# Turning the attention probabilities of twelve tiles on VectorE and through DRAM, in GpSimd's queue, in place of TensorE transposes

## The chip, the core and the metric

The kernel runs on one core of a Trainium2 chip. The metric is the device time of one execution in microseconds. Before the change the median of three timed runs is 555.21 us (554.4 to 555.64). TensorE (PE in the profile) does the products and the transposes into PSUM, VectorE (DVE) and ScalarE (ACT) empty PSUM and do the arithmetic, GpSimd (POOL) does a few copies and issues some DMAs, SyncE's queue (SP) issues nearly all the others.

## What is computed

Three stages follow each other on 2304 tokens of width 512:

```python
# 1. causal attention in a window of 64, 4 x 8 heads of 64, 576 positions
scores = (q @ k.T) / 8, masked to 0 <= i - j < 64
attn = exp(scores - max); attn /= attn.sum() + 1e-9
x = (attn @ v), heads side by side            # 2304 x 512
# 2. gated product
x = ((x @ w_a) * (x @ w_b)) @ w_out           # inner width 1536
# 3. soft mixture: 32 slots = 8 experts x 4
logits = x @ phi
d = softmax(logits, over tokens); c = softmax(logits, over slots)
slot_out[e] = relu((d.T @ x)[e] @ w1[e]) @ w2[e]
out = c @ slot_out
```

All inputs are float32 in the kernel; `w_a` and `w_b` come as 64-bit floats and are decoded on the chip.

## The kernel before

**Tiles and slots.** The tokens are 18 tiles of 128 (`NTILE`). The gated product of a tile is three units of 512 inner columns (`fg` 0, 1, 2); each unit is two slots, one for `w_a` and one for `w_b`, of 12 (or 24 half as wide) matmuls in `glu` (line 424). ScalarE copies the `a` bank out of PSUM (line 430), VectorE multiplies the `b` bank by it into `g` (line 434). There are 114 slots in all. Slots 0 to 23 are part of a start-up order that is written out as a string; from slot 24 on `run_slot` issues, slot by slot, first the events put at that slot and then the slot's `glu`. TensorE keeps exactly this order (`MANUAL`); the order on the other engines is set by the planner of the tile framework, which goes by program order and by when it reckons an instruction ready.

**Attention of tile t** is put at slots counted from `sA[t]`: queries turned and copied at s-2 and keys at s-1 (`att_q`, `att_k`), scores at s (`att_s`: 32 matmuls of line 259, then eight row minima on VectorE of line 272 and eight exponentials on ScalarE of line 279), division by the row sums at s+1 (`att_n`, line 297), the transposes of the two halves of the heads at s+2 and s+3 (`att_pt`: four TensorE transposes each, line 139 by way of the helper, and one copy out of PSUM, line 307 on ScalarE or line 309 on VectorE), and the product with the values at s+4 (`att_pv`, line 320), whose result is cast by ScalarE (line 325) and split by VectorE (line 327) into the two parts of `x` that `glu` reads. Keys of the half tile before are handed on by a GpSimd copy (line 233). The first slot of tile t's products, `first[t]`, is 6t for tiles 4 to 14, then 90, 92 and 94; `sA[t]` is the smaller of `first[t] - 6` and three slots ahead of the next tile. So tiles 5 to 14 start at 6t - 6 and tiles 15, 16, 17 at 82, 85 and 88, and the values product of each tile stands two slots ahead of the tile's first `glu` at the latest.

**Logits of tile t** are put at slots counted from `R[t]` (24 + 4t for tiles 0 to 7, 57 for tile 8, then 6 more for each tile up to 93 for tile 14). For tiles 2 to 14 `r_b` turns `g` in 32 x 32 squares on VectorE (line 452), writes it to DRAM by four SyncE DMAs (line 458) and reads it back turned by a fifth (line 463); the three parts are put at R-6, R-4 and R-3. `r_l` at R multiplies by `phi` (line 477). `r_k` at R+1 makes both forms of the logits in PSUM (`lt`, lines 497 and 499); VectorE takes their maxima (lines 501, 508 and 532) and ScalarE their exponentials `e`, `co` and `ce` (lines 511, 517 and 535). `r_d` at R+2 transposes `e` on TensorE into `dps`. `lt` and `dps` are tiles of the same single PSUM buffer (`ps_m`, tag "m"), so `dps` waits until every reader of `lt` is done, `ce` being the last. `r_u` at R+3 adds the tile to the slot inputs (line 553).

**Shared buffers.** `ps_t` tag "t" has two PSUM buffers that all transposes use. `ex1` tag "e" has three buffers of 4 KB a partition, used for staging weights at first and then by `r_b`. The project of `w_out` on `phi` in the start-up writes decoded weights to DRAM by twelve DMAs of GpSimd's queue (line 573); all of these are issued before 140 us.

Of the kernel before, what the change touches and what calls it, by code (L numbers as in the profile page):

```python
# [11 lines left out]
F32 = mybir.dt.float32  # L12
# [8 lines left out]
P = 128  # L21
# [46 lines left out]
def swa_glu_softmoe_kernel(  # L68
# [13 lines left out]
    nc = tc.nc  # L82
# [5 lines left out]
    W = 64  # L88
    NTILE = NT // P
# [7 lines left out]
    EPS = 1.0e-9  # L97
    NFIRST = 4
    NLAST = 3
    N_EX1 = 3  # L100
    N_EX2 = 7
    EARLY = 6
# [3 lines left out]
    dram = ctx.enter_context(tc.tile_pool(name="dram", bufs=1, space=bass.MemoryType.DRAM))  # L106
# [5 lines left out]
    small = ctx.enter_context(tc.tile_pool(name="small", bufs=3))  # L112
    ex1 = ctx.enter_context(tc.tile_pool(name="ex1", bufs=N_EX1))

# [23 lines left out]
    def transpose(o, i):  # L138
        nc.tensor.transpose(o, i, ident)  # L139
# [41 lines left out]
    att = att_stack.enter_context(tc.tile_pool(name="att", bufs=2))  # L181
# [116 lines left out]

    def att_pt(t, hh):
        st = sts[t]  # L300
        tp = ps_t.tile([P, 4, P], F32, tag="t", name="tp")
        for u in range(4):
            transpose(tp[:, u], st["pr"][hh][:, u])
        yield
        pT = att.tile([P, 4, P], F32, tag="pT", name="pT", bufs=3)
        if hh == 0 or t <= NFIRST:
            nc.scalar.copy(out=pT, in_=tp)  # L307
        else:
            nc.vector.tensor_copy(pT, tp)  # L309
        st["pT", hh] = pT  # L310

    def att_pv(t):
        st = sts[t]
        xps = ps_t.tile([P, 4, P], F32, tag="x", name="xps", bufs=1)
        for b in range(2):
            vt = loaded[t]["b" if b else "a"]
            c = slice(W * b, W * b + W)
            for u in range(4):
                for h in range(2):
                    nc.tensor.matmul(  # L320
                        xps[W * h:W * h + W, u, c], lhsT=vt[:, 2 * u + h, :], rhs=st["pT", h][:, u, c],
                    )
        yield
        x = xp.tile([P, 2, 4, P], F32R, tag="x", name="x")
        nc.scalar.copy(out=x[:, 0], in_=xps)  # L325
        yield
        nc.vector.tensor_tensor(out=x[:, 1], in0=xps, in1=x[:, 0].bitcast(F32), op=ALU.subtract)
        xts[t] = (x[:, 0], x[:, 1])
        del sts[t], loaded[t]


    whi, wlo = {}, {}
    wbufs = {"w0": 8, "w1": 8, "w2": 4, "w3": 4, "e": N_EX1}
    wo_dram = dram.tile([DFF, DM], F32, name="wo_dram")
# [131 lines left out]
    def bank(t, shape, nm):  # L466

        if t < NTILE - 2:
            return ps_m.tile(shape, F32, tag="m", name=nm)
        return ps_s.tile(shape, F32, tag=f"s{t % 2}", name=nm)  # L470
# [19 lines left out]
    def r_k(t):  # L490

        l4 = rst[t, "l4"]
        late = t >= NTILE - NLAST
        lt = bank(t, [P, P + NS], "lt")
# [103 lines left out]
    def both(t0, tag):  # L598

        n = min(4, NTILE - NLAST - t0) if t0 < NTILE - NLAST else NLAST  # L600
        c = p2.tile([P, 4, 4, NS], F32R, tag=tag, name="c4")
# [57 lines left out]
    def fetch(n=0):  # L659

        while nxt[0] < len(order):
            i = nxt[1] % len(slots)
            if nxt[1] >= len(slots) and slots[i][1] in ("as1", "gT1"):
                nxt[1] += 1
                continue
            if nxt[1] < len(slots):
                if n == 0:
                    return
                n -= 1
            elif not all(k in used for k in held[i]):  # L670
                return
            nxt[1] += 1
            pool, tag = slots[i]
            bufs = pool_bufs.get(tag)
            nh = slot_halves.get(tag, 2)
            x = pool.tile([P, 512 * nh], F32, tag=tag, name="xw", bufs=bufs)
            held[i] = []
            h = 0
            while h < nh and nxt[0] < len(order):
                key = order[nxt[0]]  # L680
                src, (r0, nr), (c0, ncol), pair = source(key)
                two = pair and h + 1 < nh
                if key[0] == "1":
                    ncol *= 1 + two
                else:
                    nr *= 1 + two
                nh2 = 1 + two
                nc.sync.dma_start(
                    out=x[:, 512 * h:512 * (h + nh2)].rearrange("p (c d) -> p c d", d=ncol),
                    in_=src[r0:r0 + nr, c0:c0 + ncol].rearrange("(c p) d -> p c d", p=P),  # L690
                )
                for j in range(nh2):
                    key = order[nxt[0]]
                    exw[key] = x[:, 512 * (h + j):512 * (h + j + 1)]
                    held[i].append(key)
                    nxt[0] += 1
                h += nh2

    def use(key):
        used.add(key)  # L700
        return exw[key]


    units = [(0, 0), (1, 0), (0, 1), (1, 1), (2, 0), (2, 1), (3, 0), (3, 1)] + [(t, 2) for t in range(NFIRST)]
    for t in range(NFIRST, NTILE - NLAST):
        units += [(t, fg) for fg in range(NFG)]
    LAST = range(NTILE - NLAST, NTILE)
    units += [(t, fg) for fg in range(NFG - 1) for t in LAST]
    units += [(t, NFG - 1, (h,)) for h in range(2) for t in LAST]
    NSLOT = 2 * len(units)  # L710
    events = {n: [] for n in range(NSLOT + 40)}

    def at(n, f, *a):
        events[n].append((f, a))

    first = {}
# [3 lines left out]
        done[t, fg] = 2 * i + 1  # L720
    sA = {}
    for t in range(NTILE - 1, NFIRST - 1, -1):
        sA[t] = min(first[t] - 6, sA.get(t + 1, NSLOT) - 3)
    lastA = sA[NTILE - 1] + 5
    by_squares = [t for t in range(2, NTILE - NLAST) if done[t, NFG - 1] + 2 < lastA]
    R = {}
    for t in range(NTILE - NLAST):
        R[t] = max(done[t, NFG - 1] + (4 if t in by_squares else 3), R[t - 1] + 4 if t else 24)
    for t in range(NFIRST, NTILE):
        s = sA[t]  # L730
        at(s, att_s, t)
        at(s + 1, att_n, t, 0)
        at(s + 1, att_n, t, 1)
        at(s + 2, att_pt, t, 0)
        at(s + 3, att_pt, t, 1)
        at(s + 4, att_pv, t)
        at(s - 2, att_q, t)
        at(s - 1, att_k, t)
        if t + 1 < NTILE:
            at(s, load, t + 1, "qk")  # L740
            at(s + 5, load, t + 1, "ab")
    for t in range(NTILE):
        if t < NTILE - NLAST:
            r = R[t]
# [15 lines left out]
    a, b, c = LAST  # L760
# [11 lines left out]
    def open_ex():  # L772
# [3 lines left out]
        slots.extend([(p2, "as1")] * 2 + [(p2, "gT1")] * 2)  # L776
        slots.extend([(ex1, "e")] * N_EX1 + [(exs["ex2"], "y")] * N_EX2 + [(exs["ex3"], "z")] * N_EX3 + [(gp, "g"), (xp, "x")])
        slots.extend([(wp, "w0")] * 8 + [(wp, "w1")] * 8 + [(wp, "w2")] * 4 + [(xp, "x")] + [(wp, "w3")] * 4)
        slots.extend([(xp, "x")] * 2 + [(gp, "g")] * 3)
        fetch(4 + N_EX1 + N_EX2 + N_EX3)  # L780
        for t in turns.values():
# [17 lines left out]
    def run_slot(n):  # L799
# [9 lines left out]
        "Ph": lambda _: run(nc.sync.dma_start, phi, moe2_phi.rearrange("(k p) s -> p k s", p=P)), "Ri": lambda _: build_ri(),  # L809
        "Tq": lambda t: load(t, "qk"), "Tv": lambda t: load(t, "ab"), "Aq": att_q, "Ak": att_k, "As": att_s, "An": att_n,  # L810
        "Ap": att_pt, "Av": att_pv, "Sa": partial(stage_w, "a"), "Sb": partial(stage_w, "b"),
        "Da": partial(split_w, "a"), "Db": partial(split_w, "b"), "Ga": lambda t, fg: glu(t, fg, "a"),
        "Gb": lambda t, fg: glu(t, fg, "b"), "Rt": r_t, "Po": project_phi,
# [23 lines left out]
    xps = ps_m.tile([P, DM], F32, tag="m", name="xs")  # L837
    x4 = p2.tile([P, DM], F32, tag="as0", name="x4")
    sps = ps_t.tile([P, KD, NS], F32, tag="x", name="sps", bufs=1)
    with tc.manual_schedule(engines=MANUAL):  # L840
# [16 lines left out]
        for h in range(2):  # L857
            c = slice(DM // 2 * h, DM // 2 * (h + 1))
# [14 lines left out]
    for u in range(2):  # L873
        hps = [ps_ab.tile([P, 512], F32, tag="ab"[n], name=f"h{n}") for n in range(2)]
        for kk in range(KD):
            for n in range(2):
                for e in range(4):
                    nc.tensor.matmul(
                        hps[n][32 * e:32 * e + 32], lhsT=sinT[:, kk],
                        rhs=use(("1", u, kk, e, n)),  # L880
# [129 lines left out]
```

## Time and profile before

| | |
|---|---|
| median of the timed runs | 555.21 us (554.4 to 555.64) |
| the profiled execution | 554.43 us |
| its span, first to last instruction | 552.7 us |
| TensorE busy, mean granted clock | 509.6 us (92%), 0.983 |
| VectorE, ScalarE, GpSimd busy | 310.6, 207.5, 75.5 us |
| DMA moved, mean rate | 103.48 MB, 187 GB/s |
| TensorE transposes of the probabilities, all tiles | 144, 22.7 us busy |

The profile is of one execution. Busy times of matmuls overlap each other, so the time that a group of matmuls takes of TensorE is read from the starts of the instructions around it. In the rows below a line of a timeline has the start in us, the length in us, the engine, the line of the kernel, the operation with its output and inputs, and in brackets how long the engine was idle before it and what ended that.

### The profile page before, as it was taken

To read this page: it belongs to the slowest core of one execution; us is meant where nothing else is said; L and a number is where in the kernel's file an instruction comes from. 1 tells how busy PE (TensorE), PEld (TensorE's weight loads), DVE (VectorE), ACT (ScalarE), POOL (GpSimd) and SP (SyncE) were. 2 spreads that over 40 slices of the span, in tenths; PEclk is the share of its full clock that TensorE was granted. 3 is DMA by queue.
4 is the path that set the end of the run, shared out by engine and by line. 5 is a ranking of instruction groups with operands and counts; after the bars stand their busy time and mean duration, and the time that the engine had idled before them with its cause. 6 is when DMAs were issued, how large, how long until landed. Compare 5 with 4: busy or idle time off the path is not lost.

```text
span 552.7 us, 11931 instructions
## 1 busy us (share of the span) xinstructions
PE 509.6 (92%) x4567; PEld 399.1 (72%) x4567; DVE 310.6 (56%) x888; ACT 207.5 (38%) x636; POOL 75.5 (14%) x110
## 2 busy tenths in 40 slices
PE   4588798989999999999999999999999999989993
PEld 3366576779878888787888878888787778944442
DVE  3999999996556463655646454465554311143123
ACT  5667675455534242324424232342433211132013
POOL 3555556451000000000000000000000000020000
PEclk9789899999999999999999999999999999999997
DMA  9986269565337445453525535255436899799997
GB/s 271 255 242 213 81 219 261 172 187 154 99 92 176 125 126 121 126 117 96 135 81 130 120 92 134 77 135 144 106 84 183 282 365 391 261 329 348 348 357 254
DMA packets 138904, 103.48 MB, mean 187 GB/s; under 512 B 80736, under 2 KB 121696, under 8 KB 138848
## 3 DMA queue, kind: packets, MB, share of 16 engines
q1 hardware_dynamic: 137888, 99.58, 62.1%
q0 software_dynamic: 960, 3.15, 1.5%
q8 instruction: 36, 0.59, 0.4%
q14 instruction: 20, 0.16, 0.1%
HBM read 84.61 MB, written 18.09 MB: 186 GB/s over the span
## 4 chain that ended last, share of the span: by engine, by line
PE 66%; DVE 16%; DMA 10%; issue 3%; ACT 2%; SPq 1%; ACTq 0%; DVEq 0%
PE psb L424 25%; PE psa L424 22%; DMA xw<-in_moe_w_dram 7%; PE lps L477 3%; DVE w L349 3%; PE xps L320 3%; PE ups L553 2%; DVE w L353 2%; PE s L259 2%; PE tp L139 2%; DVE w L343 2%; DVE pr L272 2%; PE tg L139 1%; DVE w L345 1%; DVE rs L291 1%
## 5 line engine op out<-in xcount | busy, mean ns | idle before, releaser
L424 PE MATMUL psb<-whb,x 128*128 128x512 f32 (+1 forms) x576 | 161.5, 349 | 1.8 <-DVE g L434 1.7
L424 PE MATMUL psa<-wha,x 128*128 128x512 f32 (+1 forms) x576 | 160.5, 347 | 2.6 <-ACT wha L397 1.6
L424 PEld LDWEIGHTS psa<-wha,x 128*128 128x128 f32 x576 | 101.5, 190 | 21.5 <-issue 5.7
L424 PEld LDWEIGHTS psb<-whb,x 128*128 128x128 f32 x576 | 101.2, 189 | 21.3 <-issue 6.9
L424 PE MATMUL psa<-wla,x 128*128 128x512 f32 (+1 forms) x288 | 97.2, 338 | 1.2 <-POOL wla L399 1.0
L424 PE MATMUL psb<-wlb,x 128*128 128x512 f32 (+1 forms) x288 | 96.8, 336 | 0.0
L434 DVE TENSOR_TENSOR g<-psb,asb 128x512 f32<-128x512 f32 (+1 forms) x57 | 37.7, 661 | 89.8 <-PE psb L424 76.8
L279 ACT ACTIVATE pr<-pr,nmx 128x128 f32<-128x128 f32 x144 | 55.8, 390 | 47.0 <-DVE nmx L272 47.0
L430 ACT COPY asb<-psa 128x512 f32<-128x512 f32 (+1 forms) x57 | 31.9, 559 | 90.7 <-PE psa L424 90.6
L424 PEld LDWEIGHTS psa<-wla,x 128*128 128x128 f32 x288 | 54.7, 190 | 6.6 <-POOL wla L399 1.7
L424 PEld LDWEIGHTS psb<-wlb,x 128*128 128x128 f32 x288 | 54.7, 190 | 4.4
L233 POOL COPY kTs<-kTs 128x256 f32<-128x256 f32 x17 | 8.2, 482 | 257.3 <-DVE kTs L244 252.7
L325 ACT CAST x<-xps 128x512 fp32r<-128x512 f32 x18 | 10.5, 583 | 50.8 <-PE xps L320 50.8
L259 PE MATMUL s<-kTs,qTs 64*64 64x128 f32 x576 | 23.7, 301 | 5.6 <-DVE nmx L272 3.1
L452 DVE STREAM_TRANSPOSE gq<-g 128x512 f32<-128x512 f32 x39 | 27.6, 708 | 1.0
L279 ACT ACTIVATION_READ_ACCUMULATOR pr<-pr,nmx 128x1 f32 x144 | 27.0, 187 | 0.0
L309 DVE COPY pT<-tp 128x512 f32<-128x512 f32 x13 | 9.0, 690 | 29.5 <-PE tp L139 29.5
L259 PEld LDWEIGHTS s<-kTs,qTs 64*64 64x64 f32 x576 | 18.2, 147 | 9.4 <-issue 4.3
L272 DVE CUSTOM_DVE_ANT_0 pr<-s,masks 128x128 f32<-128x128 f32 x112 | 24.6, 282 | 0.3 <-PE s L259 0.3
L307 ACT COPY pT<-tp 128x512 f32<-128x512 f32 x23 | 13.4, 581 | 27.7 <-PE tp L139 27.7
L139 PE MATMUL tp<-ident,pr 128*128 128x128 f32 x144 | 22.7, 281 | 0.6 <-POOL pr L297 0.6
L139 PEld LDWEIGHTS tp<-ident,pr 128*128 128x128 f32 x144 | 18.1, 144 | 5.5 <-POOL pr L297 1.7
(135 smaller groups left out, 714.0 us busy)
## 6 DMA issues: line engine op xcount, KB each, us to landing
xw<-in_moe_w_dram SPq DMA_DIRECT2D x39, 512.0 KB, 7.3
xw<-in_moe_w_dram SPq DMA_DIRECT2D x50, 256.0 KB, 6.1
gd<-gq SPq DMA_DIRECT2D x156, 64.0 KB, 2.1
gT<-gd SPq DMA_DIRECT2D x39, 256.0 KB, 2.9
st<-in_moe_w_b_dram SPq DMA_DIRECT2D x12, 512.0 KB, 5.6
st<-in_moe_w_a_dram SPq DMA_DIRECT2D x12, 512.0 KB, 5.6
st<-in_moe_w_out_dram SPq DMA_DIRECT2D x12, 512.0 KB, 5.1
out_dram<-ob SPq DMA_DIRECT2D x18, 256.0 KB, 3.2
```

Source lines behind the costliest of these rows:

```text
L139: nc.tensor.transpose(o, i, ident)
L259: nc.tensor.matmul(sps[h][c, u], lhsT=qT[r, u, c], rhs=kTs[r, t % 2, u, W * b:W * b + P],)
L272: nc.vector.tensor_tensor_reduce(out=pr[:, u].rearrange("p (a k) -> p a k", a=2), in0=sps[h][:, u].rearrange("p (a k) -> p a k", a=2), in1 ...
L279: nc.scalar.activation(out=pr[:, u], in_=pr[:, u], func=ACTF.Exp, scale=-1.0, bias=nmx[:, i:i + 1], accum_out=sm[:, i:i + 1],)
L307: nc.scalar.copy(out=pT, in_=tp)
L320: nc.tensor.matmul(xps[W * h:W * h + W, u, c], lhsT=vt[:, 2 * u + h, :], rhs=st["pT", h][:, u, c],)
L349: nc.vector.scalar_tensor_tensor(out=i, in0=hi, scalar=-(1 << 30), in1=i, op0=ALU.bitwise_and, op1=ALU.bitwise_or)
L424: nc.tensor.matmul(ps[:, cols], lhsT=l[:, kk], rhs=r, start=(n == 0), stop=(n == 3 * KD - 1))
L430: nc.scalar.copy(out=asb[:, cols], in_=ps[:, cols])
L434: nc.vector.tensor_tensor(out=gts[t][:, gcols], in0=ps[:, cols], in1=pas.pop((t, fg))[:, cols], op=ALU.mult)
L452: nc.vector.transpose(out=gq.rearrange("p (j c t) -> p c j t", j=4, c=4), in_=gts[t][:, 512 * fg:512 * fg + 512].rearrange("p (c j f) -> p ...
L477: nc.tensor.matmul(lps[32 * i:32 * i + 32].rearrange("p (i t) -> p i t", t=32) if t in by_squares else lps[32 * i:32 * i + 32], lhsT=wphi[ ...
```

## The change

A constant `NPLAIN = 6` divides the tiles. Tiles 0 to 5 keep their transposes on TensorE. For tiles 6 to 17 `att_pt` turns each half of the heads in 32 x 32 squares by one VectorE instruction into one half of a buffer `pq` (from `ex1` tag "e"). When both halves are there, four DMAs of GpSimd's queue write the buffer to a DRAM tile `pd` (32 partitions each, runs of 1 KB), and two more DMAs of the same queue, one for each half of the heads, read it back turned into `pT` (128 partitions, four runs of 512 bytes each). The values product reads `pT` with two runs of 32 columns in place of one of 64. For these tiles `sA` is two slots earlier against `first`, both calls of `att_pt` are put at s+2, the values product at s+6 in place of s+4 and the loads of the next values at s+7 in place of s+5; the end of attention, `lastA`, and the values products stay at the slots where they were.

```diff
--- before.py
+++ after.py
@@ -97,6 +97,7 @@
     EPS = 1.0e-9
     NFIRST = 4
     NLAST = 3
+    NPLAIN = NFIRST + 2
     N_EX1 = 3
     N_EX2 = 7
     EARLY = 6
@@ -298,6 +299,27 @@
 
     def att_pt(t, hh):
         st = sts[t]
+        if t >= NPLAIN:
+
+            if hh == 0:
+                st["pq"] = ex1.tile([P, 4, 2, 4, 32], F32, tag="e", name="pq")
+            pq = st["pq"]
+            nc.vector.transpose(
+                out=pq[:, :, hh].rearrange("p j u q -> p u j q"), in_=st["pr"][hh].rearrange("p u (j k) -> p u j k", j=4)
+            )
+            if hh == 0:
+                return
+            pd = dram.tile([4, 32, 4, 2 * P], F32, tag="pd", name="pd", bufs=2)
+            for i in range(4):
+                nc.gpsimd.dma_start(
+                    out=pd[:, :, i].rearrange("j k e -> k j e"),
+                    in_=pq[32 * i:32 * i + 32].rearrange("p j h u q -> p j (h u q)"),
+                )
+            for h in range(2):
+                pT = att.tile([P, 4, P], F32, tag="pT", name="pT", bufs=3)
+                nc.gpsimd.dma_start(out=pT, in_=pd[:, :, :, P * h:P * h + P].rearrange("j k i e -> (j k) i e"))
+                st["pT", h] = pT.rearrange("p i (u q) -> p u i q", u=4)
+            return
         tp = ps_t.tile([P, 4, P], F32, tag="t", name="tp")
         for u in range(4):
             transpose(tp[:, u], st["pr"][hh][:, u])
@@ -317,9 +339,13 @@
             c = slice(W * b, W * b + W)
             for u in range(4):
                 for h in range(2):
-                    nc.tensor.matmul(
-                        xps[W * h:W * h + W, u, c], lhsT=vt[:, 2 * u + h, :], rhs=st["pT", h][:, u, c],
-                    )
+                    o = xps[W * h:W * h + W, u, c]
+                    if t >= NPLAIN:
+                        o = o.rearrange("p (i q) -> p i q", i=2)
+                        r = st["pT", h][:, u, 2 * b:2 * b + 2]
+                    else:
+                        r = st["pT", h][:, u, c]
+                    nc.tensor.matmul(o, lhsT=vt[:, 2 * u + h, :], rhs=r)
         yield
         x = xp.tile([P, 2, 4, P], F32R, tag="x", name="x")
         nc.scalar.copy(out=x[:, 0], in_=xps)
@@ -720,8 +746,8 @@
         done[t, fg] = 2 * i + 1
     sA = {}
     for t in range(NTILE - 1, NFIRST - 1, -1):
-        sA[t] = min(first[t] - 6, sA.get(t + 1, NSLOT) - 3)
-    lastA = sA[NTILE - 1] + 5
+        sA[t] = min(first[t] - (8 if t >= NPLAIN else 6), sA.get(t + 1, NSLOT) - 3)
+    lastA = sA[NTILE - 1] + 7
     by_squares = [t for t in range(2, NTILE - NLAST) if done[t, NFG - 1] + 2 < lastA]
     R = {}
     for t in range(NTILE - NLAST):
@@ -732,13 +758,14 @@
         at(s + 1, att_n, t, 0)
         at(s + 1, att_n, t, 1)
         at(s + 2, att_pt, t, 0)
-        at(s + 3, att_pt, t, 1)
-        at(s + 4, att_pv, t)
+        late = 2 if t >= NPLAIN else 0
+        at(s + 2 if late else s + 3, att_pt, t, 1)
+        at(s + 4 + late, att_pv, t)
         at(s - 2, att_q, t)
         at(s - 1, att_k, t)
         if t + 1 < NTILE:
             at(s, load, t + 1, "qk")
-            at(s + 5, load, t + 1, "ab")
+            at(s + 5 + late, load, t + 1, "ab")
     for t in range(NTILE):
         if t < NTILE - NLAST:
             r = R[t]
```

## Rows read from the trace of the kernel before

**Rows 1.** Busy time of each engine by stretch (window, length, engines, clock, DMA share, GB/s).

```profile
145.00:430.00 285.00, 281.07 (x2661) 232.36 (x2661) 154.42 (x534) 97.97 (x355) 4.41 (x11) 1.00 0.47 119
```

**Rows 2.** What TensorE waited for in 150:430 (us in total, times, longest).

```profile
PE dps L139 <- ACT ce L535: 1.9, 2, 1.1
PE lps L477 <- DMA gT<-gd: 1.2, 1, 1.2
```

**Rows 3.** Instructions on the tile pr in 170:430 (ns min/median/max, first and last start).

```profile
L139 PE MATMUL tp<-ident,pr x96: 270/272/273, 180.9 to 425.4; 128*128 128x128 f32 x96
```

**Rows 4.** TensorE's timeline around the transposes of tile 10.

```profile
279.48 0.60 PE L139 MATMUL tp<-ident,pr 128*128 128x128 f32 x4
279.83 0.47 PE L424 MATMUL psa<-wha,x 128*128 128x512 f32 x1
...
282.67 0.60 PE L139 MATMUL tp<-ident,pr 128*128 128x128 f32 x4
283.19 0.86 PE L477 MATMUL lps<-gT,wphi 128*32 128x128 f32 x24
...
286.40 0.39 PE L424 MATMUL psb<-wlb,x 128*128 128x512 f32 x1
286.63 0.39 PE L424 MATMUL psb<-whb,x 128*128 128x512 f32 x1
286.95 0.69 PE L320 MATMUL xps<-pT,lda 128*64 128x64 f32 x16
```

**Rows 5.** Costliest groups of the page (busy us, mean ns | idle before).

```profile
L452 DVE STREAM_TRANSPOSE gq<-g 128x512 f32<-128x512 f32 x39 | 27.6, 708 | 1.0
L309 DVE COPY pT<-tp 128x512 f32<-128x512 f32 x13 | 9.0, 690 | 29.5 <-PE tp L139 29.5
```

**Rows 6.** DMAs through DRAM: GpSimd's (issue ns, us to landing), SyncE's (KB, us to landing).

```profile
L573 POOL DMA_DIRECT2D wo_dram<-wo x12: 539/568/1770, 62.9 to 139.7; - x12
DMA to landing us min/median/max: 2.4/4.1/8.5
...
gd<-gq SPq DMA_DIRECT2D x156, 64.0 KB, 2.1
gT<-gd SPq DMA_DIRECT2D x39, 256.0 KB, 2.9
```

**Rows 7.** Slots 52 and 54 on TensorE; the end of tile 10's division on VectorE.

```profile
264.96 0.39 PE L424 MATMUL psa<-wha,x 128*128 128x256 f32 x1
...
272.91 0.48 PE L424 MATMUL psa<-wha,x 128*128 128x512 f32 x1
...
277.59 0.68 DVE L297 TENSOR_TENSOR pr<-pr,rs 128x512 f32<-128x512 f32 x1
```

**Rows 8.** Timeline of slots 82 and 83: scores, `lt`, exponentials, `dps`.

```profile
383.48 1.10 PE L259 MATMUL s<-kTs,qTs 64*64 64x128 f32 x32
384.51 0.49 PE L497 MATMUL lt<-l,ri 128*128 128x128 f32 x2
...
387.94 0.60 PE L139 MATMUL tq<-ident,ldq 128*128 128x128 f32 x4
...
389.23 0.28 ACT L535 ACTIVATE ce<-lt,rm 128x32 f32<-128x32 f32 x1
...
389.66 0.33 PE L139 MATMUL dps<-ident,e 128*128 128x128 f32 x1 [1.13 <-ACT ce L535]
```

**Rows 9.** TensorE's timeline at slot 89.

```profile
417.80 0.33 PE L139 MATMUL dps<-ident,e 128*128 128x128 f32 x1 [0.77 <-ACT ce L535]
```

**Rows 10.** Timeline at slots 37 and 38: `ce` and the transposes ahead of `dps`.

```profile
205.12 0.29 ACT L535 ACTIVATE ce<-lt,rm 128x32 f32<-128x32 f32 x1
...
205.64 0.60 PE L139 MATMUL tp<-ident,pr 128*128 128x128 f32 x4
```

**Rows 11.** One issue of GpSimd's queue in the start-up, and VectorE beside it.

```profile
95.86 1.77 POOL L573 DMA_DIRECT2D wo_dram<-wo  x1 [3.12 <-DVE wo L353]
...
96.08 0.41 DVE L343 TENSOR_SCALAR w<-w 128x512 f32<-128x512 f32 x1
```

## The prediction

> **What bounds the kernel now.** I read the table by stretch first. From 145 to 430 us, which holds all the attention that the change touches, TensorE is busy 281.07 of 285.00 us at a granted clock of 1.00; VectorE is busy 154, ScalarE 98, GpSimd 4, the DMA engines 0.47 [rows 1]. The reader is to see that one engine has no gaps and the others have many. Then I read what TensorE waited for there: the two largest entries are 1.9 us on `dps` and 1.2 us on `lps` [rows 2]. So in this stretch a microsecond taken out of TensorE's order is a microsecond of the span, and one more wait is one lost. What follows 430 us starts from slot 93, where attention ends in both kernels; it moves with it. All sums are made against the profiled execution, 554.43 us, of which the span is 552.7; the median of the runs is 0.78 above it, and I add that at the end.
>
> **Removed: transposes on TensorE.** For tiles 6 to 17, 96 matmuls on `pr` go, in 24 groups of four [rows 3]. A group's busy time overlaps, so I take starts. The group at 279.48 is followed by the next product at 279.83: 0.35 us. The one at 282.67 is followed by `lps` at 283.19: 0.52, but a change from the product to such an f32 group costs 0.09 anyway (the step from 286.63 to 286.95 is 0.32, the ordinary step from 286.40 is 0.23), so 0.43 is saved [rows 4]. Five of the 24 groups are followed directly by a product, the others by another f32 group: 5 x 0.35 + 19 x 0.43 = 9.9 us. TensorE has no gap that could swallow this: **-9.9**.
>
> **Copies and squares.** 24 copies out of PSUM go, half on ScalarE, half on VectorE at 690 ns; 24 turns on VectorE come, bounded by the same shape's 708 ns [rows 5]: net 12 x (2 x 0.71 - 0.69) = 8.8 us more on VectorE, in a stretch where it idles 130 us [rows 1]. At nothing for the sum; it is VectorE's order that can cost, below. The values product reads runs of 32 columns; the `lps` group reads `gT` in the same manner and 24 of its matmuls take 0.8 us [rows 4], so nothing.
>
> **Added: the way through DRAM.** The trace has GpSimd issues of 128 runs only: 0.54 us each at the quickest, landing 2.4 to 8.5 us after, median 4.1 in the busy start-up. SyncE's nearest transfers land in 2.1 (writes of 64 KB from 32 partitions) and 2.9 us (the turned read of 256 KB) [rows 6]. The chain from the end of the division: two turns 1.42; four writes issued 0.54 apart, the last landed 2.4 to 4.1 after its issue, 4.0 to 5.7; two reads, each issue between 0.54 and four times that for its 512 runs (2.16), the last landing 2.9 to 4.1 after its own: 3.4 to 6.3. Together **8.9 to 13.4 us**, nearest to the lower end, since the DMA share is 0.47. If the planner puts a `g` product and a `gq` turn first (0.69 + 0.71), 1.4 more. The cover: tile 10's division ends at 278.27 [rows 7], its values product starts at 286.95 [rows 4], 8.7 us; two slots more (264.96 to 272.91, 7.95) [rows 7], less the 0.8 of removed transposes: **15.8 us**. Tiles 15 to 17 stand only three slots apart, some 12 us, but from the first write's issue to the last read's GpSimd needs at most 5.7 + 2 x 2.16 = 10 of them. So the reads are hidden by the products of four slots, 1 us to spare in the worst sum. Behind the waiting GpSimd issues stands only the copy of the next keys (line 233), which is ready before them. The buffers "e" are asked for four times in six slots and held 4 to 8 us each: three suffice.
>
> **Moved: scores two slots earlier.** This is where I expect loss. New starts are 6t - 8 = 28 to 76 for tiles 6 to 14, then 80, 83, 86. `r_k` of tile t' stands at R+1 = 6t' + 10 from tile 8 on. These meet at slots 58, 64, 70 and 76: scores and logits in one slot. Before, that happens at 82 and 88. What it costs is seen at 82: scores at 383.48, `lt` behind them; VectorE does eight minima before the maxima of `lt`, ScalarE eight exponentials before `e` and the copy of the `a` bank before `ce` (389.23), and only then can `dps` use the buffer: it starts at 389.66, 1.13 us idle behind four query transposes that began at 387.94 [rows 8]. In the new places nothing stands between the product and `dps` (queries are then at s-2, two slots after), so the loss is the whole 389.66 - 387.94 = 1.72. The rest of the slot is alike (the values product stands at 82 too). **+4 x 1.72 = +6.9**; bounds 0.77, the smaller wait, at slot 89 [rows 9], and 2.3 with the key copy or a turn before it. The two old waits, 1.13 and 0.77 [rows 8, 9], go, as no tile now starts at 82 or 88: **-1.9**.
>
> Three more places (slots 28, 40, 52) have the logits one slot after the scores, as slot 37 has now. There `ce` ends at 205.41 and `dps` would be due, without the transposes ahead of it, at 205.64 [rows 10]: 0.2 us to spare. The values product's split (0.69) now comes before the minima at all three, and a turn of `pq` (0.71) fits in front of the last maximum. Bounds 0 and 1.3 each; I take the middle, as either alone exceeds the margin: **+3 x 0.7 = +2.1**.
>
> **Sum:** 554.43 - 9.9 + 6.9 - 1.9 + 2.1 = 551.6; with 0.78 for the median, **552.4 us**. With the bounds (4 x 0.77 to 4 x 2.3; 0 to 3.9) the same case runs from 546.5 to 556.5.
>
> **Rival 1, the new waits do not form.** ScalarE's order is the planner's; if it puts `ce` ahead, or the maxima ahead of the minima, only the removals stay: 554.43 - 9.9 - 1.9 + 0.78 = 543.4. For it: at slot 38 before, the same chain just fits. Against it: at 82 and 88 the same planner made exactly this wait. Chance 0.16.
>
> **Rival 2, the reads come late and the kernel is slower.** Mechanism: the values product (line 320) waits for `pT`, with all TensorE behind it. It decides from a chain of 15.8 us; the forecast's gain of 2.8 over nine tiles (6 to 14) is gone 0.3 us later. Price: one issue in the start-up took 1.77 us [rows 11] where the others take 0.54; at 1.77 for all six and landings of 4.1 the chain is 1.4 + 3 x 1.77 + 4.1 + 1.77 + 1.77 + 4.1 = 18.5, so 2.7 us late in each of nine tiles: 552.4 + 24 = 576. At one such issue and the rest as in the upper sum nothing is late. For it: no run of 512 pieces is in the trace. Against it: that issue ran beside a row of 0.41-us TENSOR_SCALARs on VectorE (the first of them at 96.08) [rows 11], which the stretch from 145 on does not have; and the cover is near twice the lower sum. Chance 0.14.
>
> The Trainium skill ("SBUF — State Buffer", Who interferes with whom) speaks against putting these DMAs on GpSimd: a VectorE copy or TENSOR_SCALAR in its two-port mode shuts GpSimd out for the whole instruction, descriptor writing included, and it advises another queue. By that rule the 1.77 us is explained, and the trace agrees; on VectorE the stretch from 145 us on has such instructions between SBUF tiles on at most 32 columns, so by the rule the issues stay near 0.54 and the sum does not move.
>
> **Rival 3, `lps` waits for its own way through DRAM.** For tiles 8 to 12 `r_b` of the last part stands at R-3 = 54 to 78, the very slots of the new `att_pt`. Two turns (1.42) ahead of `gq`, and 512 KB written and 512 KB read beside `gd` and `gT`, use up a margin of some 3 us. The one such wait in the trace is 1.2 us [rows 2]; five of them give 552.4 + 6 = 558.4, one or two leave it near 555. Chance 0.17.
>
> **How the numbers follow.** Forecast 0.53, rivals 0.16, 0.14, 0.17. A measurement of this kernel can tell about 0.2%, so below 554.1 is faster and above 556.3 slower. Faster: 0.41 of the forecast's 0.53 (554.1 lies some three quarters up its range), rival 1's 0.16, 0.04 of rival 3: 0.61. Same: 0.09 of the forecast, 0.05 of rival 3, 0.01 of rival 2: 0.15. Slower: 0.03, 0.08 and 0.13 of the same three: 0.24. The range: the forecast's bounds with rival 3's full price above, and below down to rival 1 with two of four waits left (545): **545 to 560**. Left out are the rest of rival 1 and nearly all of rival 2, 0.2.
>
> **What would show it.** Right: 48 matmuls on `pr` in place of 144; TensorE's waits led by `dps <- ACT ce`, at four places around 290 to 370 us, 1 to 2 us each; GpSimd's last read landed 2 us or more ahead of line 320, which waits for nothing; six GpSimd issues a tile, the writes near 0.5 us. Wrong: `xps <- DMA pT` among TensorE's waits (rival 2), `lps <- DMA gT` several times (rival 3), no `dps` wait at all (rival 1), or VectorE's turns so late that a `b` bank is not emptied and `psb` waits for line 434.

## The result, and the profile after

The changed kernel takes 549.15 us (547.72 to 549.72) where the kernel before, beside it, takes 554.81 (552.97 to 555.64): a ratio of 0.991, interval 0.989 to 0.993. Measured a second time it was 0.9925, 0.990 to 0.995. The kernel is faster by 4 to 6 us; the forecast was 2.8, with the range 545 to 560.

The profiled execution took 547.72 us, its span is 545.9. Its line numbers are higher than before's: the values product is line 348 (320 before), the logits' product on `gT` 503 (477), `ce` 561 (535); the transpose into `dps` is called in line 569 and recorded at line 140.

The stretch of [rows 1], 5 us shorter, in the table by stretch of the kernel after (window, length, PE, PEld, DVE, ACT and POOL busy with counts, granted clock, DMA share, GB/s):

```profile
145.00:425.00 280.00, 270.98 (x2556) 221.88 (x2555) 159.19 (x547) 90.46 (x341) 48.80 (x83) 1.00 0.64 167
```

GpSimd went from 4 to 49 us and the DMA share from 0.47 to 0.64, the granted clock stayed 1.00. TensorE, which idled 4 us of 285, now idles 9 of 280. What it waited for there, against [rows 2]:

```profile
PE dps L140 <- ACT ce L561: 6.4, 4, 1.6
PE lps L503 <- DMA gT<-gd: 1.6, 2, 1.3
PE psb L450 <- DVE g L460: 0.8, 1, 0.8
```

The four long waits of the forecast are there, and nothing waits for `pT`. The transposes left on `pr` in this stretch, against the 96 of [rows 3] (ns min/median/max, first and last start):

```profile
L140 PE MATMUL tp<-ident,pr x8: 270/272/273, 153.6 to 158.5; 128*128 128x128 f32 x8
```

The costliest groups of the kernel after (busy us, mean ns | idle before), where [rows 6] had only issues of 128 runs, and the landing of its transfers (KB, median us):

```profile
L314 POOL DMA_DIRECT2D pd<-pq x48 | 26.4, 558 | 120.4 <-DVE cst L565 48.0
L320 POOL DMA_DIRECT2D pT<-pd x24 | 18.0, 756 | 40.0 <-DMA pd<-pq 32.0
...
gT<-gd SPq DMA_DIRECT2D x39, 256.0 KB, 3.3
gd<-gq SPq DMA_DIRECT2D x148, 64.0 KB, 2.7
pd<-pq POOLq DMA_DIRECT2D x48, 128.0 KB, 3.2
pT<-pd POOLq DMA_DIRECT2D x24, 256.0 KB, 3.9
```

The `cst` that is named before the writes ends 0.13 us after the turn that they read; the issue follows 0.3 us behind that turn. A read's issue of 512 runs takes 0.76 us, near the lower bound (0.54 to 2.16). Its landing (3.9) is in the forecast's 2.9 to 4.1, the writes' (3.2) in 2.4 to 4.1. The older transfers, [rows 6] 2.1 and 2.9 us, now take 2.7 and 3.3.

The chain of tile 10, from timelines of the kernel after (start, length):

```profile
264.89 0.68 DVE L298 TENSOR_TENSOR pr<-pr,rs 128x512 f32<-128x512 f32 x1
265.61 0.71 DVE L307 STREAM_TRANSPOSE pq<-pr 128x512 f32<-128x512 f32 x1
266.62 2.20 POOL L314 DMA_DIRECT2D pd<-pq  x4 [10.79 <-DVE rm L558]
271.79 1.50 POOL L320 DMA_DIRECT2D pT<-pd  x2 [2.98 <-DMA pd<-pq]
281.51 0.69 PE L348 MATMUL xps<-pT,lda 128*64 128x64 f32 x16
```

The division ends at 265.57, the last packet of the second read lands at 276.38: 10.8 us, and 5.1 more until the product asks. Over the twelve tiles the chain takes 10.1 us (tile 13) to 14.7 (tile 14), and 2.1 us (tile 17) to 7.8 (tile 12) are left over. The semaphore that tells of the landing follows 0.5 to 0.7 us behind the last packet, so by it 1.6 to 7.2 us are left.

**Where the time is.** The first product of slot n is a mark that all these kernels have. Its start, in us from the start of the span, from the timelines of TensorE:

| kernel | slot 24 | 30 | 54 | 78 | 93 | 113 | 24 to 113 |
|---|---|---|---|---|---|---|---|
| before | 148.53 | 174.30 | 272.91 | 368.44 | 433.54 | 483.05 | 334.52 |
| after | 147.16 | 172.96 | 267.46 | 368.20 | 427.34 | 476.85 | 329.69 |
| c_after | 147.39 | 173.18 | 267.70 | 369.04 | 427.97 | 477.48 | 330.09 |
| e1_shift_only | 147.89 | 174.12 | 272.08 | 374.07 | 436.19 | 485.70 | 337.81 |
| e2_late_d | 148.68 | 174.47 | 268.99 | 365.52 | 425.77 | 475.29 | 326.61 |
| e8_late_logits_four | 147.08 | 172.87 | 267.42 | 356.97 | 416.84 | 466.35 | 319.27 |
| e9_before_late_logits | 148.38 | 174.13 | 272.74 | 366.50 | 432.56 | 482.07 | 333.69 |

Of the 6.8 us between the two spans, 1.4 lie ahead of slot 24, which the change doesn't touch, and 0.6 behind slot 113. Between these marks the change gains 4.8 us, and 4.4 in its second profile (c_after). By parts: up to slot 54 it gains 4.1, from 54 to 78 it gives back 5.2, up to 93 it gains 6.0 (at 78 it has the four query transposes of tile 15 behind it, 0.4 us, which the kernel before has in the last part). The middle part holds the four meetings.

### The profile page after: what moved, and what is told of

It is laid out like the page before. It is cut to its first block, busy times and chain, and to the rows that moved or that the text cites. A ratio compares the mean times of both kernels' runs of the same rounds, so it can differ in the third digit from the quotient of the medians.

```text
span 545.9 us, 11859 instructions
## 1 busy us (share of the span) xinstructions
PE 499.8 (92%) x4471; PEld 388.9 (71%) x4471; DVE 314.6 (58%) x900; ACT 200.9 (37%) x624; POOL 119.9 (22%) x182
## 4 chain that ended last, share of the span: by engine, by line
PE 70%; DVE 18%; issue 3%; DMA 3%; ACT 3%; SPq 1%; POOL 0%; POOLq 0%; ACTq 0%
PE psb L450 26%; PE psa L450 20%; PE ops L939 3%; PE xps L348 3%; DVE w L375 3%; PE lps L503 3%; PE h L905 2%; DVE pr L273 2%; PE ups L579 2%; DVE w L379 2%; DMA gT<-gd 2%; DVE w L369 2%; PE s L260 2%; PE tg L140 1%; DVE w L371 1%
## 5 line engine op out<-in xcount | busy, mean ns | idle before, releaser
L314 POOL DMA_DIRECT2D pd<-pq x48 | 26.4, 558 | 120.4 <-DVE cst L565 48.0
L320 POOL DMA_DIRECT2D pT<-pd x24 | 18.0, 756 | 40.0 <-DMA pd<-pq 32.0
L245 DVE COPY kTs<-tk 128x512 f32<-128x512 f32 x13 | 9.0, 690 | 22.7 <-PE tk L140 22.7
L369 DVE TENSOR_SCALAR w<-w 128x512 f32<-128x512 f32 x24 | 16.3, 679 | 8.9 <-ACT w L367 8.9
```

Source lines behind the costliest of these rows:

```text
L314: nc.gpsimd.dma_start(out=pd[:, :, i].rearrange("j k e -> k j e"), in_=pq[32 * i:32 * i + 32].rearrange("p j h u q -> p j (h u q)"),)
L320: nc.gpsimd.dma_start(out=pT, in_=pd[:, :, :, P * h:P * h + P].rearrange("j k i e -> (j k) i e"))
L369: nc.vector.tensor_scalar(out=t, in0=t, scalar1=DBL_LO, scalar2=DBL_HI, op0=ALU.max, op1=ALU.min)
```

## The experiments

Each edit is made to the changed kernel, where nothing else is said. Ratios are to the kernel before, run beside it on the same chip.

### The changed kernel again

> The changed kernel again, unaltered, as the level that the other three of this call are compared with. Both theories expect its ratio to the kernel before near 0.991, about 549 us.

549.16 us (546.91 to 550.46), ratio 0.9925 [0.990, 0.995]. Its waits are those above, but for `lps`: 2.3 us in three.

### The slots alone

```diff
-        if t >= NPLAIN:            # in att_pt and in att_pv
+        if t >= NTILE:
...
-        at(s + 2 if late else s + 3, att_pt, t, 1)
+        at(s + 3, att_pt, t, 1)
```

The scores stand two slots earlier, but every tile keeps its transposes on TensorE.

> The earlier scores alone: probabilities keep their TensorE transposes in all tiles, but tiles 6 to 17 start two slots earlier and the values product stands six slots after the scores. Theory (the shift makes logits and scores meet at slots 58, 64, 70 and 76, and dps waits there for ce): slower than the kernel before by 4 x 1.6 less the two old waits of 1.9, so by 4 to 5 us, ratio 1.008, with about 6.4 us of dps <- ce among TensorE's waits. Rival (the waits are made by the new turns and DMA issues, not by the shift): within 1 us of the kernel before, dps waits of 2 us or less.

556.76 us, ratio 1.006 [1.0045, 1.008]: slower than the kernel before. TensorE's waits in this kernel, 145 to 430 us:

```profile
PE dps L140 <- ACT ce L561: 6.3, 4, 1.6
PE psb L450 <- DVE g L460: 0.8, 1, 0.8
```

The same four waits, though no probability goes through DRAM: they come from the slots. The `lps` waits of the kernel after are not here, nor is that of [rows 2]: with the slots as they are, it is the new way that makes them, by its turns on VectorE or by its traffic; no run parts the two. Against this kernel the way through DRAM is worth 7.6 us by the clock (556.76 - 549.16). In the trace it is 8.1 (337.81 - 329.69), and 9.7 if the 1.6 us of `lps` waits are added back; 7.7 and 10.0 with c_after. The forecast's sum for the groups was 9.9.

### `dps` one slot later where it meets scores

```diff
+    starts = set(sA.values())
...
-            at(r + 2, r_d, t)
-            at(r + 3, r_u, t)
+            d = r + 1 in starts
+            at(r + 2 + d, r_d, t)
+            at(r + 3 + d, r_u, t)
```

> The changed kernel with the transpose into dps and the update that follows it one slot later for the tiles whose logits meet a tile's scores (tiles 8 to 11). Theory (the four waits are worth what the trace shows): 6.4 us less than the changed kernel, so 543 us and a ratio near 0.979, no dps wait left. Rival (the wait only moves: line 579 or the next tile's lps stands behind it): within 1.5 us of the changed kernel, with as much waiting on another row.

545.44 us, ratio 0.986 [0.984, 0.988]: 3.7 us less than the changed kernel, not 6.4. The `dps` waits are gone, and another has grown. Its waits, and the timeline at slot 69:

```profile
PE lps L503 <- DMA gT<-gd: 4.3, 3, 3.0
...
327.95 0.43 PE L503 MATMUL lps<-gT,wphi 128*32 128x128 f32 x8 [3.02 <-DMA gT<-gd]
```

The table by stretch of this kernel shows what came behind that wait (the column after POOL is the granted clock):

```profile
300.00:324.00 24.00, 24.00 (x215) 19.81 (x214) 12.57 (x42) 6.83 (x26) 4.10 (x7) 1.00 0.65 159
329.00:332.40 3.40, 3.40 (x10) 2.66 (x9) 0.00 (x0) 0.00 (x0) 0.00 (x0) 0.51 0.27 78
332.40:350.00 17.60, 17.60 (x163) 14.73 (x163) 11.59 (x40) 6.24 (x25) 3.70 (x6) 1.00 0.51 126
```

For 3.4 us TensorE ran at 0.51, its lower level of 1.2 GHz, which makes the wait dearer by some 1.7 us, half of that time. So 6.4 us were taken out, and 2 us more of `lps` (4.3 against 2.3 in c_after) and 1.7 of clock came in: 2.7 left in that sum, 3.5 in the trace (330.09 - 326.61). By the starts of the matmuls the four waits are 7.0 and not 6.4, as worked out below; that makes it 3.3. The waits for the bank and those for `gT` are two margins a few us apart: what TensorE no longer idles, `gT` no longer has.

### Another PSUM buffer for `dps`

```diff
-        dps = bank(t, [P, P], "dps")
+        dps = ps_t.tile([P, P], F32, tag="t", name="dps") if t in by_squares else bank(t, [P, P], "dps")
```

> The changed kernel with dps of tiles 2 to 14 in the buffers of the transposes (ps_t, tag t) in place of the one it shares with lt; the order is kept. Theory (dps waits for the buffer, whose last reader is ce, not for its input e): in the changed kernel's slot 59 e ends at 287.74, ce at 288.66, and the product ahead of dps ends near 287.2, so of each 1.6 us about 0.9 goes: 3 to 4 us less than the changed kernel, 545.5 us, and the rest is waited for on e. Rival (e itself, behind the eight exponentials, is the whole wait): no gain, 549 us.

545.62 us, ratio 0.987 [0.984, 0.989]: 3.5 us less than the changed kernel. Its waits:

```profile
PE dps L140 <- ACT e L537: 2.6, 4, 0.7
PE lps L503 <- DMA gT<-gd: 2.6, 2, 1.8
```

With a buffer of its own `dps` waits for its operand `e`, 0.7 us, where it waited 1.6 for the buffer that `ce` holds. So the buffer is a little over half of each wait, and the late exponentials are the rest.

### Logits and `r_b` one slot apart from the scores, all late tiles

```diff
+        more = 8 <= t < NTILE - NLAST - 1
-        R[t] = max(done[t, NFG - 1] + (4 if t in by_squares else 3), R[t - 1] + 4 if t else 24)
+        R[t] = max(done[t, NFG - 1] + (4 + more if t in by_squares else 3), R[t - 1] + 4 if t else 24)
...
-                    at(max(done[t, fg] + 1, r - (6, 4, 3)[fg]), r_b, t, fg)
+                    at(max(done[t, fg] + 1, r - (6, 4, 3)[fg] - (8 <= t < NTILE - NLAST - 1)), r_b, t, fg)
```

`r_k`, `r_d` and `r_u` of tiles 8 to 13 go one slot later; `r_b` keeps its slots and so has one slot more for `gT`.

> The changed kernel with the logits of tiles 8 to 13 one slot later (R = 6t + 10), while the three parts of g are turned at the slots where they were. Logits then stand one slot behind a tile's scores, as at slots 29, 41 and 53, where the changed kernel's trace has no wait, and lps has one slot more to wait for gT. Theory (both remaining waits, 6.4 us on dps and 1.6 to 2.3 us on lps, come from where these events are put, not from the new path): 8 us less than the changed kernel, 541 us, with neither row among TensorE's waits. Rival (the places behind the scores are near misses that cost 0.7 us each, as the prediction had it): six of these give 4 us back, 545 us, with dps waits of some 0.7 us.

539.61 us, ratio 0.975 [0.973, 0.977]. One wait of `dps` is left (1.0 us, at slot 84, where the moved logits of tile 12 now meet the scores of slot 83), and 0.6 us of `lps`. The logits of four tiles stand one slot behind scores here, and none of them waits: this near meeting costs nothing.

### The same for tiles 8 to 11 alone

```diff
+        more = 8 <= t < 12
```

(and the same condition in `r_b`).

> The changed kernel with the logits of tiles 8 to 11 alone one slot later; tiles 12 and 13 stay at R = 81 and 87. With tiles 8 to 13 moved, one dps wait of 1.0 us was left, at slot 84, where tile 12's logits had been moved onto tile 16's scores at slot 83. Theory (every such meeting costs, and only these): that wait goes, nothing comes in its place, 1 us less than with six tiles moved, 538.6 us. Rival (tiles 12 and 13 need the slot for gT): lps waits of 1 us or more at slots 81 and 87, the same time or more, 539.5 to 541 us.

538.47 us (537.87 to 539.11), ratio 0.973 [0.971, 0.975]: **10.7 us less than the changed kernel**. Its interval overlaps that of the last experiment; in the traces it is 2.1 us below it from slot 24 to 113 (319.27 against 321.35), 1.6 of them waits. Its waits and its stretch, and `dps` of the tile whose wait in the changed kernel is the row at 288.81 below:

```profile
PE psb L450 <- DVE g L460: 0.8, 1, 0.8
PE lps L503 <- DVE dt L571: 0.4, 1, 0.4
...
145.00:425.00 280.00, 278.67 (x2630) 229.11 (x2629) 162.40 (x558) 94.93 (x350) 48.92 (x83) 1.00 0.67 177
...
289.55 0.28 PE L450 MATMUL psb<-whb,x 128*128 128x256 f32 x1
289.67 0.27 PE L140 MATMUL dps<-ident,e 128*128 128x128 f32 x1
```

TensorE idles 1.3 us of 280, against 9 in the changed kernel, and its records hold 74 matmuls more for the same time. Here `dps` starts without a wait, 0.12 us after the start of the matmul ahead of it.

### The same on the kernel before

The edit of the last experiment, made to the kernel before, which keeps its transposes and its slots.

> The kernel before, TensorE transposes and all, with the logits of tiles 8 to 11 one slot later. It tells how much of the gain with late logits is the way through DRAM. Theory (before, nothing met at these slots): only the 1.2 us of lps at slot 69 goes, ratio 0.998, 552 us, so the way through DRAM is worth 9.9 us and a little when nothing meets. Rival (late logits help either kernel by about as much): 545 us or less.

552.89 us, ratio 0.999 [0.9975, 1.0005]: no change that can be told from nothing; in the traces it is 0.8 us (334.52 - 333.69). Its waits of TensorE:

```profile
PE dps L139 <- ACT ce L535: 1.9, 2, 1.1
PE psb L424 <- DVE g L434: 0.8, 1, 0.8
```

The wait for `gT` of [rows 2] is gone, the two for `dps` stay. So the late logits are worth about nothing by themselves. They are worth 10.7 us behind the change, because the change made the meetings. Between this kernel and e8 stands the whole of the change with nothing in its way: 14.4 us (552.89 - 538.47), and 14.4 in the traces too (333.69 - 319.27).

### The way through DRAM in the old slots

```diff
-        sA[t] = min(first[t] - (8 if t >= NPLAIN else 6), sA.get(t + 1, NSLOT) - 3)
-    lastA = sA[NTILE - 1] + 7
+        sA[t] = min(first[t] - 6, sA.get(t + 1, NSLOT) - 3)
+    lastA = sA[NTILE - 1] + 5
...
-        late = 2 if t >= NPLAIN else 0
-        at(s + 2 if late else s + 3, att_pt, t, 1)
+        late = 0
+        at(s + 2 if t >= NPLAIN else s + 3, att_pt, t, 1)
```

> The changed kernel's way through DRAM on the slots of the kernel before: scores at first - 6, both turns at s+2, the values product at s+4. Theory (the chain needs 10 to 14 us and the two extra slots are its cover): in the changed kernel the last read ends 2.1 to 7.8 us ahead of the values product, 53 us over the twelve tiles, and two slots are about 8 us, so the product comes 12 x 8 - 53 = 42 us late in all; four dps waits go (6.4) and two come back (1.9): 549 + 38 = 587 us, xps waiting for the DMA into pT at nearly every tile. Rival (the cover is more than needed and the earlier scores only cost): 545 us, no such wait.

613.89 us, ratio 1.109 [1.105, 1.114], 27 us more than expected. This is rival 2 made real. Its waits over the whole run, one of them in the timeline, and the stretch behind it:

```profile
PE xps L348 <- DMA pT<-pd: 45.7, 22, 6.6
...
222.21 0.47 PE L348 MATMUL xps<-pT,lda 128*64 128x64 f32 x2 [3.73 <-DMA pT<-pd]
...
221.00:227.80 6.80, 4.97 (x61) 3.89 (x61) 0.69 (x1) 1.18 (x2) 0.00 (x0) 0.50 0.61 157
227.80:251.00 23.20, 21.57 (x173) 17.52 (x173) 14.26 (x50) 6.88 (x29) 4.10 (x7) 1.00 0.51 133
```

The waits are 46 of the 65 us by which it is longer than the changed kernel: a longer and a shorter one at each of eleven tiles. With ten of the longer ones (2.5 to 6.6 us) the clock goes to the lower level for 3.4 or 6.8 us, beginning within the wait or up to 1.3 us behind it, in ten stretches between 190 and 487 us. TensorE is busy for 47 us of these; at half speed some 24 of them are lost. The `dps` waits that go (6.4 in the changed kernel, 0.5 here) stand against that, and with them the sum is 64. The two slots that the change gives are needed.

### The six DMAs in SyncE's queue

```diff
-                nc.gpsimd.dma_start(      # writes of pd; the same for the reads of pT
+                nc.sync.dma_start(
```

> The changed kernel with the twelve tiles' six DMAs in SyncE's queue, with gd and gT, in place of GpSimd's. Theory (the queue's order matters: the reads of pT wait some 3 us for their writes and the writes wait for the turns, and gd, gT and the loads of the next tiles stand behind them): lps waits for gT at most tiles from 6 on, 1 to 2 us each, 5 to 15 us more than the changed kernel. Rival (issue by SyncE is quicker, 0.4 us and not 0.56 and 0.76, and lands sooner, and all of it is hidden anyway): within 1 us of the changed kernel or faster.

568.29 us, ratio 1.0285 [1.025, 1.032]: 19 us more than from GpSimd. TensorE's waits, two transfers as they land, and what SyncE's queue itself waited for, 145 to 440 us:

```profile
PE lps L503 <- DMA gT<-gd: 11.5, 6, 3.1
PE dps L140 <- ACT ce L561: 6.3, 4, 1.6
...
pd<-pq SPq DMA_DIRECT2D x48, 128.0 KB, 2.7
pT<-pd SPq DMA_DIRECT2D x24, 256.0 KB, 3.4
...
SPq L314 <- DVE cst L565: 11.9, 4, 4.1
SPq L320 <- DMA pd<-pq: 8.2, 12, 2.1
SPq L314 <- DVE pq L307: 8.1, 2, 5.2
```

Each transfer lands 0.5 us sooner than from GpSimd (2.7 and 3.4 against 3.2 and 3.9), and the kernel is slower. The queue goes in order: it stands 28 us (11.9 + 8.2 + 8.1) for the squares and for its own writes, and the writes and reads of `gd` stand behind. That makes `lps` wait 11.5 us, and with four of these waits the clock is at its lower level for 3.4 us each. One more wait, 1.9 us, is for the queries of a tile, whose load is in the same queue. The Trainium skill ("DMA: Bandwidth & Descriptors", Issuing engine by pattern) calls the hardware queues generally faster, and the landings agree. Here it is what a queue holds up that decides.

### Each half of the heads by itself

Each half writes its own four DMAs of 64 KB and reads as soon as it is turned, eight writes and two reads a tile in place of four and two:

```diff
-            if hh == 0:
-                return
-            pd = dram.tile([4, 32, 4, 2 * P], F32, tag="pd", name="pd", bufs=2)
             for i in range(4):
                 nc.gpsimd.dma_start(
-                    out=pd[:, :, i].rearrange("j k e -> k j e"),
-                    in_=pq[32 * i:32 * i + 32].rearrange("p j h u q -> p j (h u q)"),
+                    out=pd[hh, :, :, i].rearrange("j k e -> k j e"),
+                    in_=pq[32 * i:32 * i + 32, hh].rearrange("p j u q -> p j (u q)"),
...
-            for h in range(2):
+            for h in (hh,):
```

> The changed kernel with each half of the heads on its own: four writes of 64 KB and one read as soon as a half is turned, in place of four writes of 128 KB and two reads when both are. Theory (the chain is hidden by 2 us or more at every tile): the same time within 0.3%, though GpSimd issues ten DMAs a tile and not six. Rival (the waiting first read holds GpSimd's second half back, or twice the small writes crowd the DMA engines): values products late at the tiles with the least to spare, 6, 7 and 17, or more waits on gT: 3 us or more slower.

550.62 us, ratio 0.996 [0.994, 0.998]; that of the changed kernel, 0.9925 [0.990, 0.995], overlaps it. The `dps` waits are the same 6.4 us, `lps` 1.7, and `pT` is waited for once, 0.2 us. GpSimd is busy 70 us in place of 49. By the medians both halves at once is worth 0.3%, by the traces 0.15 to 0.55 us from slot 24 to 113, and these runs can't tell it from nothing.

## What the prediction had right, and the term that failed

**What bounds the kernel:** right. Every change of the time here is a change of what TensorE does or waits for, or of its clock. VectorE's extra work cost nothing: no wait for `g` came with it, the one `psb` wait of 0.8 us is in e9 too.

**The way through DRAM and its cover:** right. The chain takes 10.1 to 14.7 us where 8.9 to 13.4 were worked out, and 1.4 more with other work of VectorE in front; the slots cover it with 2.1 us or more to the last packet. With two slots less, 22 waits come (e5). The forecast's cover of 15.8 us is that of tile 10: 10.8 + 5.1 in the rows above.

**The terms of the sum**, by the rows of the kernel after and of e1 (recorded idle time of TensorE for the waits):

| term | forecast | measured | from |
|---|---|---|---|
| 24 groups of transposes gone | -9.9 | -9.7 (-10.0) | after (c_after) against e1, with the `lps` waits added back |
| four new meetings | +6.9 | +6.4 | waits of `dps` |
| two old meetings gone | -1.9 | -1.9 | no such wait left |
| three near meetings | +2.1 | 0 | no wait at slots 30, 42, 54 |
| `lps` waits for `gT` | rival 3 | +0.4 (+1.1) | 1.6 (2.3) against 1.2 in [rows 2] |
| sum | -2.8 | -4.8 (-4.4) | slots 24 to 113: -4.8 (-4.4) |

**The step that failed is the near meetings.** The prediction took 0.7 us each for slots 28/29, 40/41 and 52/53, because a split of the values product before the minima and a turn in front of the last maximum (`rm`) would each be longer than the 0.2 us to spare in that chain [rows 10]. The three measure 0; without them its sum is -4.9. Both instructions stood where it feared them. Rows of the kernel before at slots 37 and 38, then rows of the kernel after around slots 41 and 42:

```profile
202.42 0.38 PE L497 MATMUL lt<-l,ri 128*128 128x128 f32 x2
...
204.89 0.19 DVE L532 TENSOR_REDUCE rm<-lt 128x1 f32<-128x32 f32 x1 [0.59 <-ACT e L511]
...
216.86 0.39 PE L523 MATMUL lt<-l,ri 128*128 128x128 f32 x2
...
218.82 0.71 DVE L307 STREAM_TRANSPOSE pq<-pr 128x512 f32<-128x512 f32 x1
218.94 0.37 ACT L537 ACTIVATE e<-lt,nm 128x128 f32<-128x128 f32 x1 [1.30 <-DVE nm L534]
219.45 0.17 DVE L558 TENSOR_REDUCE rm<-lt 128x1 f32<-128x32 f32 x1
219.66 0.29 ACT L561 ACTIVATE ce<-lt,rm 128x32 f32<-128x32 f32 x1
220.18 0.27 PE L140 MATMUL dps<-ident,e 128*128 128x128 f32 x1
```

The turn runs while ScalarE makes `e`, and for `e` VectorE had idled 0.59 us ahead of `rm` in the kernel before. The split, too, found room: the last minimum ends at 215.2, 1.7 us ahead of `lt`. From `lt` to the end of `ce` it takes 3.09 us (219.95 - 216.86), where it took 2.99 at slots 37 and 38 (205.41 - 202.42), and `ce` ends 0.23 us ahead of `dps`: the same 0.2 to spare as before. At slots 29 and 53 a turn (of `gq` and of `pq`) stands ahead of `rm` as well, and `dps` doesn't wait. So the prediction added the whole length of an instruction to a chain in which that engine had idle time.

**The new meetings** were right in place, cause and price. One of them in the kernel after:

```profile
282.59 1.10 PE L260 MATMUL s<-kTs,qTs 64*64 64x128 f32 x32
...
286.93 0.28 PE L450 MATMUL psa<-wha,x 128*128 128x256 f32 x1
...
287.39 0.35 ACT L537 ACTIVATE e<-lt,nm 128x128 f32<-128x128 f32 x1
288.38 0.28 ACT L561 ACTIVATE ce<-lt,rm 128x32 f32<-128x32 f32 x1
288.81 0.33 PE L140 MATMUL dps<-ident,e 128*128 128x128 f32 x1 [1.60 <-ACT ce L561]
```

The recorded idle time is 1.60, where 1.72 was read off slot 82 by starts [rows 8]. By starts it is 1.76 here: in e8 `dps` follows 0.12 us after the start of the matmul ahead of it, so it is due at 287.05. The next matmul can start before the recorded end of the one ahead (0.28 long, 0.12 apart), so a wait costs some 0.16 us more than its recorded idle time, and the four cost 7.0. By e3 it is `ce` on the shared buffer for 0.9 of it and the late `e` for 0.7.

**Rival 3** came in small. It had five waits, the kernel after has two, 0.4 us more than before in sum. It is the next margin: e2, which takes only the `dps` waits away, meets it at once. **Rival 1** (no new waits, 543.4) didn't happen, but e8 makes it by hand, at 538.5 us, 5 us below its price. **Rival 2** needs e5's slots; no issue of the change took longer than 0.78 us, where its price went by 1.77.

**What stays open.** From e9 to e8, with nothing met on either side but the two old waits (1.9), the change is worth 14.4 us, 2.6 more than the 9.9 + 1.9 of the terms. Some of it shows between slots 30 and 54, where none of these kernels has a wait of those kinds. Four tiles are turned there: 98.61 us before and 97.96 in e1, which only moves the scores, so 0.16 a tile from the order of the work alone; 94.52 in c_after, so 0.86 a tile from the way through DRAM (0.83 in the forecast). Twelve times 0.16 is 1.9 us. That groups of the same kind now stand next to each other in a slot, so that TensorE changes between them less often, would make such a gain, but no run tries it. In the kernel after it doesn't show in the sum, since the meetings cost more than their recorded idle time: e1 is 6.5 us longer than before from slot 54 to 78, 0.4 of it the query transposes of tile 15, although the 1.2 us of [rows 2] are gone. So the four are worth 7.2 there with 6.3 of idle, and the 0.16 us a wait from above are most of the difference, which is about as large as what the order gains in e1.

## What to carry to other kernels

Work that is taken from the bounding engine shows its full price only if the slots that it needs don't put other chains on top of each other: the slots cost 3.8 us here (e1), the way through DRAM brought 7.6, and an edit of two lines that moves the four meeting logits by a slot made the change worth 15 us in place of 4 to 6. After such a move list which steps now share a slot and which buffers they share, and shift the step with slack; take two margins that lie near each other (here the bank and `gT`) apart together, since freeing one alone lets the other bite. An instruction that falls into a chain with little to spare is priced by what exceeds the idle time that its engine has there, not by its whole length, and transfers that wait for a late operand belong in a queue where nothing urgent stands behind them.

## What was not expected of the hardware

- A wait of TensorE of 3.0 us was followed by 3.4 us at a granted clock of 0.51 (e2); with the longer waits of e5, 2.5 to 6.6 us, came stretches of 3.4 or 6.8 us at 0.50. The waits of 1.6 us and less in the kernel after left the clock of 145 to 425 us at 1.00. Between these the length alone doesn't tell: in e6 waits of 1.65 and 1.71 us were followed by 3.4 us at the lower level, one of 1.74 was not, nor was one of 1.80 in e3. A long wait was thus dearer than its idle time: in e2 by some 1.7 us.
- A read of 512 runs took GpSimd 0.756 us to issue, a write of 128 runs 0.558: four times the runs, 1.35 times the time.
- The start of slot 24 lies between 147.1 and 148.7 us in the kernels of the table, without an order by kernel: two profiles of the changed kernel differ by 0.2, the kernel before and the changed one, alike up to there, by 1.4. A difference of 2 us between two spans is therefore read from marks behind the start-up.
